# Blocks for B's input and for the compared matrices, and the order in which they are loaded, in a concatenated GFNet and FNet kernel

## The chip, the cores and the metric

The kernel runs on one core of a Trainium2 chip. The metric is device time in microseconds (us) of one launch; the median of three runs of the kernel before is 220.95 us (220.74 to 221.11). A profile is one further execution, taken by the hardware profiler; its instructions are counted from the start of its span.

Engine names are those of the profile: PE is the matrix engine, DVE the vector engine, ACT the scalar engine, POOL and SP the other two; SP issues most loads and stores here. Each engine works its instructions off in the order in which they were put, and an instruction that waits holds back those behind it. "PEld" is the loading of weights, "PEq" or "SPq" an engine's sequencer, where issues and waits stand.

## The reference

Two outputs are computed and put side by side (S = 2048, D = 512):

```
A:  X = rfft2(A_x);  y = irfft2(X * (w_r + i w_i))
B:  a = x @ hid_re.T;  b = x @ hid_im.T
    y = seq_re @ a - seq_im @ b
out = concat([A, B], axis=-1)
```

The four matrices of B (two of 2048 x 2048, two of 512 x 512) are inputs. The kernel takes B's output from fast Fourier steps, and reads the given matrices whole to compare them with tables of cosines and sines; only if they differ does it compute B from the matrices themselves, in a branch that is not taken here. Nearly half of all bytes that it moves, 33.6 MB, are those two large matrices ("C").

## The kernel before, in words

Three pieces of work are written as generators, and a loop at the end of the main function weaves them.

**A** (`a_work`) is the backbone; its yields count the steps n = 0 to 62.

- Steps 0 to 11, `forward`: eight loads of A's x (512 KB each) into the region `zv`; DVE adds and subtracts mirrored halves (`folded`, through the helper `TT`, line 233); PE transforms along the hidden axis (`hidden`, 32 matmul records for the first two, 16 for each later one), ACT copies (`taken`, line 481), PE transforms along 16 rows (`along`, 4 records each), ACT copies (line 488) into one of three buffers, and POOL stores them turned into `zv` (line 492, `turned`). A third-next copy has to wait until the store from its buffer has landed.
- Steps 12 to 38: eight slots (`slot`), each in four stages: the weights' load (POOL, line 302, issued behind the last turned store) and DVE sums `t` from `zv`; two transforms on PE with a table out of `slots`; five large DVE instructions; and four transforms back with copies into `zv` (line 592). A slot's first stage needs the turned stores landed. The first to run are slot 0's and slot 1's, at step 12.
- Steps 39 to 62, `inverse`: 128 matmul records for the hidden axis, 128 for the rows, ACT copies, and four stores `out_a` of 1 MB (line 626), two after each half.

**B** (`b_work`) has 27 steps, k = 0 to 26: 0 and 1 load x in four quarters of 1 MB, 2 to 9 are a fold on DVE (`b_fold`, four instructions) and 16 matmuls (`b_along`, four groups of rows) for each quarter in turn, 10 to 18 `b_hidden`, 19 to 26 `b_rows` with two stores of 256 KB each (a plain one from SP, an indexed one from POOL, line 432) out of two buffers `yb`. `B_AT[k]` is the step of A after which step k is written. Where k is in `PINNED`, its matmuls are put behind A's latest one on PE; its loads and DVE instructions are not.

**C** (`all_compared`) has 34 steps: 16 blocks, two steps for the hidden matrices (each with one block that ACT fills and one that is loaded), 16 blocks. A block is 1 MB in two loads (line 332), then one or two DVE instructions that compare and add up (`count`, line 317). The tables `tt` (1 MB each, line 327) serve eight blocks each; halfway through its eight blocks a table gets its sign turned on DVE (line 340). `C_AT` says for a block behind which step of A its count is put on DVE: behind the last `TT` of that step. In the loop of the kernel before, block i has the entry i - 1, and block 0 none; an entry of 0 is no pin. Loads are not pinned; each is issued when its place in SP's order and a free block allow.

x of B and C's blocks share six blocks (`XR = 6`, `block()`, line 304).

The order of each engine's instructions is fixed at compile time by a list scheduler, which takes what was written first wherever it counts it ready; so what is written later can be put into gaps of what was written earlier.

At the end DVE sums all counts (line 715), PE adds over partitions (717), DVE writes a flag (718) and all engines branch on it (720, 721).

Of the kernel before, what the change touches and what calls it, by code (L numbers as in the profile page):

```python
# [10 lines left out]
F32 = mybir.dt.float32  # L11
# [5 lines left out]
P = 128  # L17

YB = 2
XR = 6  # L20


B_AT = [0, 5, 7, 7, 8, 9, 9, 9, 9, 11, 13, 13, 13, 13, 13, 18, 20, 20, 21, 23, 27, 31, 31, 32, 50, 50, 50]
C_AT = [0, 0, 0, 3, 7, 12, 12, 12, 13, 34, 34, 38, 40, 40, 40, 40, 40, 40, 40, 40, 41, 41, 41, 44, 44, 44, 45, 45, 48, 48, 50, 59, 59, 59, 59, 61]
PINNED = [1, 2, 3, 4, 5, 6, 7, 8, 9, 10, 11, 12, 13, 14, 15, 17, 21]
SMALL = 2.0**-27
TINY = 2.0**-111

# [179 lines left out]
def kernel(  # L208
# [19 lines left out]
    nc = tc.nc  # L228
# [18 lines left out]
    bp = first.enter_context(tc.tile_pool(name="bp", bufs=1))  # L247
# [8 lines left out]
    slots = ap.tile([P, 2816], F32, name="slots")  # L256

    def short():
        return ap.tile([P, 6400], F32, name="zb")
# [13 lines left out]
    fb = bp.tile([P, 2, 272], F32, name="fb")  # L273
# [21 lines left out]
    def load(dst, src):  # L295
        loads.append(nc.sync.dma_start(dst, src))
        return dst

    def late(dst, src):

        with tc.issue_after(turned[-1].ins):
            nc.gpsimd.dma_start(dst, src)  # L302

    def block():
        return bp.tile([P, 4, 512], F32, name="xr", bufs=XR)

    hts = []
# [34 lines left out]
    def hidden_table():  # L342

        if not hts:
            hts.append(nc.sync.dma_start(ht, tabs["ht"]))
# [14 lines left out]

    def b_load(q):

        x = block()
        for k in range(4):
            g = 4 * q + k
            lo, hi = 1 + 4 * g, 124 - 4 * g
            load(x[:, k], bass.AP(xb.tensor, xb.offset + 16 * D * lo, [[D, 64], [16 * D * (hi - lo), 2], [1, D]]))
        if q == 3:
            load(x[1:32:2, 3], xb[0])
        return x  # L370
# [286 lines left out]

    def b_work():
        x = {0: b_load(0)}
        yield  # L660
        x.update({q: b_load(q) for q in range(1, 4)})
        nc.gpsimd.dma_start(fb, tabs["fb"])
        yield
        for q in range(4):
            ev = b_fold(x[q])
            yield
            for g in range(4 * q, 4 * q + 4):
                b_along(g, x[q], ev)
            if q == 0:
                nc.sync.dma_start(hc, tabs["hc"])  # L670
                nc.sync.dma_start(slots, tabs["slot"])
                hidden_table()
                nc.sync.dma_start(mb, tabs["mb"])
            yield
        z = short()
        zb = [part(z, 2 * k, 512) for k in range(9)]
        for e in range(9):
            b_hidden(e, zb)
            yield
        for o in range(8):  # L680
            b_rows(o, zb)
            yield
# [7 lines left out]

    count(same[:, 0:1], same[:, 1:2], TINY, ALU.is_equal)
    a, b, c = a_work(), b_work(), all_compared()
    done = []
    b_at, c_at = list(B_AT), list(C_AT)
    while b_at and b_at[0] < 0:
        b_at.pop(0)
        next(b)
    for n in range(100):
        if next(a, a) is a and not b_at:
            break  # L700
        while b_at and b_at[0] <= n:
            b_at.pop(0)
            k = len(B_AT) - len(b_at) - 1
            with tc.issue_after(mma[0].ins) if k in PINNED else ExitStack():
                next(b, None)
        done.append(last[0])
    for _ in b:
        pass
    for _ in c:
        n = c_at.pop(0) if c_at else 0  # L710
        pin[0] = done[min(n, len(done) - 1)] if n else None


    rs = bp.tile([P, 1], F32, name="rs")
# [124 lines left out]
```

## Time and profile before

| | |
|---|---|
| median of three runs | 220.95 us |
| the profiled execution | 220.61 us, of which its span 218.6 us |
| PE, DVE, ACT, POOL busy | 192.2, 158.9, 77.2, 39.2 us |
| moved by DMA | 69.68 MB, 319 GB/s over the span |
| mean granted PE clock | 0.929 |

What lies around the span (2.0 us in the profiled execution) is launch and end. A row of the timeline gives start, duration, engine, line, operation, tiles, shape and a count; in brackets the idle time of the engine before it and who ended that. A row of a group gives busy time and mean duration. A window row gives for each engine its busy time and number of instructions, then the granted clock, the DMA engines' busy share, and GB/s.

### The profile page before, as it was taken

How to read it: one execution, taken by the hardware profiler on the slowest of the kernel's cores; microseconds unless marked ns; L12 is line 12 of the kernel's file. 1: busy time of each engine (PE TensorE's matmuls, PEld its weight loads, DVE VectorE, ACT ScalarE, POOL GpSimd, SP SyncE). 2: the span in 40 equal slices, each digit the busy share in tenths (PEclk: the TensorE clock that was granted, in tenths of full speed). 3: DMA queues.
4: the chain of work that ended last, by engine and by line, in shares of the span. 5: the costliest groups of instructions: out<-in, count | busy, mean ns of one | idle time of the engine just before them, and what ended most of it. 6: DMA issues, size and time to landing. Idle time of an engine off the chain costs nothing. (4 is left out here: it accounts for less than half of the span.)

```text
span 218.6 us, 2541 instructions
## 1 busy us (share of the span) xinstructions
PE 192.2 (88%) x833; PEld 150.0 (69%) x833; DVE 158.9 (73%) x257; ACT 77.2 (35%) x159; POOL 39.2 (18%) x56
## 2 busy tenths in 40 slices
PE   7799999979959999999999967668999999999700
PEld 2687778858749576586866544466999998888600
DVE  1589400088684899999889979799994799989350
ACT  2034333083452224422416535447333133333300
POOL 4002220032270010232113443160050000000000
PEclk9999999999995699999999996767999999999985
DMA  6999999999999999972353274057899999999990
GB/s 215 389 408 387 379 401 403 404 408 390 381 387 384 385 408 406 391 231 89 116 194 105 97 280 178 16 189 288 338 418 411 416 408 407 410 411 420 388 393 13
DMA packets 20883, 69.68 MB, mean 319 GB/s; under 512 B 3616, under 2 KB 4000, under 8 KB 19456
## 3 DMA queue, kind: packets, MB, share of 16 engines
q1 hardware_dynamic: 16176, 58.05, 67.6%
q0 software_dynamic: 4400, 10.81, 14.1%
q10 hardware_dynamic: 288, 0.59, 0.7%
q8 instruction: 8, 0.13, 0.2%
q14 instruction: 11, 0.09, 0.1%
HBM read 56.85 MB, written 8.39 MB: 298 GB/s over the span
## 5 line engine op out<-in xcount | busy, mean ns | idle before, releaser
L317 DVE SCALAR_TENSOR_TENSOR xr<-xr,tt 128x1024 f32<-128x1024 f32 (+1 forms) x24 | 37.3, 1578 | 27.9 <-DMA xr<-in_cm 27.8
L317 DVE SCALAR_TENSOR_TENSOR xr<-xr,odd,tt 128x1024 f32<-128x1024 f32 (+1 forms) x24 | 38.7, 1637 | 6.0 <-DMA xr<-in_cm 6.0
L448 PE MATMUL pa<-ye,zv 128*128 128x256 f32 x128 | 30.3, 401 | 2.0 <-ACT zv L592 2.0
L448 PE MATMUL pa<-zb,sda 128*128 128x256 f32 x128 | 30.6, 395 | 1.4 <-DVE sda L233 1.4
L448 PEld LDWEIGHTS pa<-ye,zv 128*128 128x128 f32 x128 | 29.2, 306 | 3.0 <-ACT zv L592 2.3
L448 PEld LDWEIGHTS pa<-zb,sda 128*128 128x128 f32 x128 | 25.2, 199 | 8.6 <-DVE sda L233 2.3
L233 DVE TENSOR_TENSOR sda<-zv 128x512 f32<-128x512 f32 (+1 forms) x24 | 19.0, 821 | 12.8 <-DMA zv<-in_xa 7.2
L448 PE MATMUL pa<-ye,sda 128*128 128x256 f32 x128 | 27.8, 379 | 0.0
L448 PEld LDWEIGHTS pa<-ye,sda 128*128 128x128 f32 x128 | 24.3, 190 | 3.3
L448 PEld LDWEIGHTS pa<-slots,sda 128*128 128x128 f32 x128 | 19.6, 225 | 8.5 <-DVE sda L233 3.7
L448 PE MATMUL pa<-slots,sda 128*128 128x128 f32 (+1 forms) x128 | 21.2, 328 | 2.6 <-DVE sda L233 2.6
L233 DVE TENSOR_TENSOR sda<-sda 128x512 f32<-128x512 f32 (+1 forms) x34 | 22.9, 716 | 0.0
L492 POOL DMA_DIRECT2D zv<-zb x16 | 10.0, 631 | 48.7 <-ACT zb L488 32.9
L233 DVE TENSOR_TENSOR sda<-pa,sda 128x1024 f32<-128x1024 f32 (+1 forms) x16 | 17.8, 1152 | 0.5
L481 ACT COPY zb<-pa 128x1024 f32<-128x1024 f32 x8 | 8.1, 1012 | 25.8 <-PE pa L448 25.8
L432 POOL DMA_INDIRECT out_b<-yb,turn x8 | 12.4, 1554 | 25.0 <-ACT yb L422 23.9
L448 PE MATMUL pa<-zb 128*128 128x512 f32 x32 | 15.1, 598 | 1.2 <-ACT zb L481 1.2
L388 PE MATMUL pb<-fb,xr 128*128 128x128 f32 (+1 forms) x64 | 15.4, 327 | 0.5 <-DVE xr L233 0.5
L622 ACT COPY zv<-pa 128x512 f32<-128x512 f32 x16 | 9.4, 587 | 17.8 <-PE pa L448 17.8
L302 POOL DMA_DIRECT2D sda<-in_wa x16 | 11.4, 717 | 23.0 <-ACT zb L405 10.1
L388 PE MATMUL pb<-fb,yb 128*128 128x72 f32 x64 | 13.3, 295 | 2.4 <-DVE yb L233 1.4
L611 ACT COPY sda<-pa 128x1024 f32<-128x1024 f32 x8 | 8.1, 1016 | 19.2 <-PE pa L448 19.2
(83 smaller groups left out, 216.0 us busy)
## 6 DMA issues: line engine op xcount, KB each, us to landing
xr<-in_cm SPq DMA_DIRECT2D x64, 512.0 KB, 10.3
tt<-tab_tt SPq DMA_DIRECT2D x4, 1026.0 KB, 12.6
zv<-in_xa SPq DMA_DIRECT2D x8, 512.0 KB, 9.7
xr<-in_xb SPq DMA_DIRECT2D x16, 256.0 KB, 6.9
zv<-zb POOLq DMA_DIRECT2D x16, 256.0 KB, 8.4
sda<-in_wa POOLq DMA_DIRECT2D x16, 256.0 KB, 3.7
out_a<-zv SPq DMA_DIRECT2D x4, 1024.0 KB, 10.8
xr<-in_wd SPq DMA_DIRECT2D x2, 1024.0 KB
```

The source lines that it names most:

```text
L233: last[0] = nc.vector.tensor_tensor(**kw)
L302: nc.gpsimd.dma_start(dst, src)
L317: nc.vector.scalar_tensor_tensor(raw, raw, scale, v, op0=MUL, op1=op, accum_out=stat[:, i : i + 1])
L388: nc.tensor.matmul(bank[:, at : at + hi - lo], v[:, cols], f[:, lo:hi], start=True, stop=True)
L432: stores.append(nc.gpsimd.indirect_dma_start(out=out_b, out_offset=bass.IndirectOffsetOnAxis(ap=turn[:, o : o + 1], axis=0), in_=y[:, 1], ...
L448: mma[0] = nc.tensor.matmul(*args, **kw)
L481: nc.scalar.copy(zs[p], pd[p])
L492: turned.append(nc.gpsimd.dma_start(zv[at : at + 29 : 4], ys[:, k]))
L611: nc.scalar.copy(u[:, g : g + 2], pu)
L622: nc.scalar.copy(ob[:, c, :, :, g // 2], po.rearrange("p k r s -> p r k s"))
```

## The change

- Blocks: C's pool `xr` has four blocks, and a pool `xq` has two. B's x takes `xq` alone. From the 21st block that C asks for (count 20), every third (20, 23, 26, ...) comes from `xq` as well.
- B's loads: quarter 0 is loaded at step k = 0 (with the table `fb` on POOL's queue), quarter 1 at k = 1, quarters 2 and 3 after the matmuls of quarters 0 and 1. Steps k = 0 and 1 are written after A's steps 5 and 6 instead of 0 and 5.
- C: its first two steps (table 0, blocks 0 and 1) are written after A's step 0, so ahead of x of B, with no pin. Block i now has the entry i of `C_AT`.
- `slots` is loaded by the loop after step 6, ahead of quarter 1; it was among B's tables, which stay behind quarter 0's matmuls.
- All three lists are other ones.

```diff
-XR = 6
-B_AT = [0, 5, 7, 7, 8, 9, 9, 9, 9, 11, 13, 13, 13, 13, 13, 18, 20, 20, 21, 23, 27, 31, 31, 32, 50, 50, 50]
-C_AT = [0, 0, 0, 3, 7, 12, 12, 12, 13, 34, 34, 38, 40, 40, 40, 40, 40, 40, 40, 40, 41, 41, 41, 44, 44, 44, 45, 45, 48, 48, 50, 59, 59, 59, 59, 61]
-PINNED = [1, 2, 3, 4, 5, 6, 7, 8, 9, 10, 11, 12, 13, 14, 15, 17, 21]
+XR = 4
+XQ = 2
+EARLY = 2
+LENT = 20
+SLOTS = 6
+B_AT = [5, 6, 6, 13, 13, 13, 13, 14, 14, 15, 15, 17, 17, 22, 22, 24, 24, 25, 25, 29, 29, 33, 33, 33, 40, 44, 51]
+C_AT = [0, 0, 12, 12, 13, 14, 15, 15, 15, 22, 34, 34, 34, 34, 35, 35, 35, 37, 37, 37, 37, 37, 37, 37, 43, 43, 43, 43, 43, 43, 43, 43, 43, 43, 43, 43]
+PINNED = [0, 1, 2, 7, 11, 12, 13, 14, 15, 16, 17, 18, 19, 20, 21, 22, 24, 25, 26]
...
+    blocks = [0]
     def block():
+        i = blocks[0]
+        blocks[0] += 1
+        if i >= LENT and i % 3 == 2:
+            return bp.tile([P, 4, 512], F32, name="xq", bufs=XQ)
         return bp.tile([P, 4, 512], F32, name="xr", bufs=XR)
...
     def b_load(q):
-        x = block()
+        x = bp.tile([P, 4, 512], F32, name="xq", bufs=XQ)
...
     def b_work():
         x = {0: b_load(0)}
+        nc.gpsimd.dma_start(fb, tabs["fb"])
         yield
-        x.update({q: b_load(q) for q in range(1, 4)})
-        nc.gpsimd.dma_start(fb, tabs["fb"])
+        x[1] = b_load(1)
         yield
         for q in range(4):
             ev = b_fold(x[q])
             yield
             for g in range(4 * q, 4 * q + 4):
                 b_along(g, x[q], ev)
+            if q < 2:
+                x[q + 2] = b_load(q + 2)
             if q == 0:
                 nc.sync.dma_start(hc, tabs["hc"])
-                nc.sync.dma_start(slots, tabs["slot"])
                 hidden_table()
                 nc.sync.dma_start(mb, tabs["mb"])
             yield
...
+    early = 0
     for n in range(100):
         if next(a, a) is a and not b_at:
             break
+        if n == SLOTS:
+            nc.sync.dma_start(slots, tabs["slot"])
+        while early < EARLY and c_at[0] <= n:
+            c_at.pop(0)
+            early += 1
+            next(c)
         while b_at and b_at[0] <= n:
...
-    for _ in c:
+    while early < EARLY:
+        c_at.pop(0)
+        early += 1
+        next(c)
+    while True:
         n = c_at.pop(0) if c_at else 0
         pin[0] = done[min(n, len(done) - 1)] if n else None
+        if next(c, c) is c:
+            break
```

Each step k of B, with the step of A after which it is written:

| k | what | before | after |
|---|---|---|---|
| 0, 1 | loads of quarter 0; of 1 to 3 (after: of 1) | 0, 5 | 5, 6 |
| 2, 4, 6, 8 | folds | 7, 8, 9, 9 | 6, 13, 13, 14 |
| 3, 5, 7, 9 | matmuls of the quarters | 7, 9, 9, 11 | 13, 13, 14, 15 |
| 10 to 18 | `b_hidden` | 13 (five), 18, 20, 20, 21 | 15, 17, 17, 22, 22, 24, 24, 25, 25 |
| 19 to 26 | `b_rows` | 23, 27, 31, 31, 32, 50, 50, 50 | 29, 29, 33, 33, 33, 40, 44, 51 |

The counts' pins, by block: before, blocks 0 to 3 none, 4 step 3, 5 step 7, 6 to 8 step 12, 9 step 13, 10 and later step 34 and later. After: 0 and 1 none, 2 and 3 step 12, 4 step 13, 5 step 14, 6 to 8 step 15, 9 step 22, 10 and later step 34 and later. Step 12's last `TT` is in slot 1's sums `t`, step 34's in slot 7.

## The prediction

> **What bounds the kernel now.** I read the chain of waits first, to see what ends last, and then the engines by stretches of time.
>
> ```profile
> 163.16 11.49 DMA xr<-in_cm
> ...
> 195.32 12.45 DMA xr<-in_cm
> ...
> 207.88 2.40 DVE xr L317 x4
> ...
> 210.99 0.16 DVE flag L718
> ```
>
> The last 45 us are loads of C, one behind the other; the last lands at 207.8, its count ends at 210.28, the flag at 211.15. The span ends at 218.6, 7.45 us behind the flag. So C's last landing plus 10.8 us is the span. The same window holds A's inverse:
>
> ```profile
> 0.00:72.06 72.06, 65.21 (x296) 50.14 (x297) 35.45 (x59) 25.43 (x62) 15.45 (x28) 0.95 1.00 380
> 72.06:142.80 70.74, 65.06 (x265) 42.68 (x264) 65.37 (x122) 27.50 (x61) 17.91 (x26) 0.93 0.60 222
> 95.00:147.50 52.50, 45.80 (x202) 31.55 (x200) 47.74 (x91) 22.15 (x45) 18.09 (x22) 0.90 0.42 149
> 147.50:207.80 60.30, 57.89 (x256) 53.48 (x256) 50.59 (x64) 22.04 (x33) 3.00 (x1) 0.97 0.98 391
> 72.06 1.29 DVE L233 TENSOR_TENSOR sda<-zv 128x512 f32<-128x512 f32 x2 [3.81 <-issue]
> 142.72 0.18 DVE L233 TENSOR_TENSOR sda<-sda,sg 128x2 f32<-128x2 f32 x1
> 142.80 2.35 DVE L317 SCALAR_TENSOR_TENSOR xr<-xr,odd,tt 128x2048 f32<-128x2048 f32 x1
> ```
>
> The columns are PE, weight loads, DVE, ACT, POOL, clock, DMA share, GB/s. I split where DVE's work changes: 72.06 is the first slot sum, which needs A's turned rows; 142.80 is the end of the last slot's sums, where the counts that are pinned there start. Before 72 DMA is full (1.00) and DVE half idle. From 72 to 143, the slots, DVE is busy 65.37 of 70.74 us, PE 65.06, and from 95 on DMA only 0.42: all six blocks are full and nobody has counted them. Behind 147.5 DMA is at 0.98, 391 GB/s. So what happens after 142.8 is a fixed amount of traffic, and the time of the kernel hangs on when DVE has finished the slots. Call that S; S = 142.8, C's last landing is S + 65.0, the span S + 75.8.
>
> **What DVE has to do up to S, and when.**
>
> ```profile
> 23.04 1.30 DVE L233 TENSOR_TENSOR xr<-xr 128x1020 f32<-128x1020 f32 x2
> 44.67 2.29 DVE L317 SCALAR_TENSOR_TENSOR xr<-xr,tt 128x2048 f32<-128x2048 f32 x1 [20.34 <-DMA xr<-in_cm]
> 57.90 0.70 DVE L340 TENSOR_SCALAR tt<-tt 128x1024 f32<-128x1024 f32 x1
> L233 DVE TENSOR_TENSOR yb<-yb,pb 128x255 f32<-128x255 f32 x14 | 5.2, 414 | 2.6 <-ACT yb L419 2.6
> ```
>
> DVE stands idle for 20.3 us, from 24.3 to 44.67, because the first block of C queues behind x of B. By 142.8 it has done 35.45 + 65.37 = 100.8 us of work and idled 42.0. Within that: A's folds, four folds of B, blocks 0 to 9, the slots, and seven rows of B at 5.2 / 7 = 0.74 us. Ten blocks are counted by S in both versions (the pins of block 10 and later are at step 34 or later, those of 0 to 9 at 22 or earlier); of the rows of B, five instead of seven are written before step 34, which takes 1.5 us off: 99.3 us of work. S is then 99.3 us plus DVE's idle time, and as far as S decides, the change gains only if that idle time, 42.0 us now, stays below 43.5.
>
> The order does the opposite of what the first 20 us suggest. Before, blocks 0 to 5 are counted ahead of the slots (the pins are none, 3 and 7). After, only 0 and 1 are; 2 to 9 are pinned to step 12 or later, and step 12's last DVE sum is slot 1's, the instruction group at 72.06. So four counts of 2.35 us move from the idle stretch into the busy one, with one turn of a table's sign (0.70). Of the four folds of B (two rows like that at 23.04, 2.5 us), at least one moves too: quarter 2 is loaded only when quarter 0's matmuls have freed a block of the two, and quarter 3 after quarter 1. I take one, bounds one and two. The slots' stretch holds 65.37 - 1.5 + 4 x 2.35 + 0.70 + 2.5 = 76.5 us of DVE's work. Its idle time was 5.4 us; more counts are there to fill it, three rows of B in one step (33) on two buffers make some: 4.5 us, bounds 0 and 5.4. The stretch lasts 81.0 us instead of 70.7.
>
> **When the slots can start.** A's forward part no longer has matmuls of B written into it.
>
> ```profile
> 15.36 1.88 PE L448 MATMUL pa<-zb 128*128 128x512 f32 x4
> 17.08 3.62 PE L448 MATMUL pa<-zb,sda 128*128 128x256 f32 x16
> 20.53 1.88 PE L448 MATMUL pa<-zb 128*128 128x512 f32 x4
> 53.12 3.65 PE L448 MATMUL pa<-zb 128*128 128x512 f32 x8
> 47.26 3.54 POOL L492 DMA_DIRECT2D zv<-zb  x6 [17.15 <-ACT zb L488]
> 59.82 1.01 ACT L488 COPY zb<-pa 128x1024 f32<-128x1024 f32 x1 [0.71 <-DMA zv<-zb]
> 61.12 1.19 POOL L492 DMA_DIRECT2D zv<-zb  x2 [2.38 <-ACT zb L488]
> DMA to landing us min/median/max: 7.2/8.4/11.6
> ```
>
> The period is 20.53 - 15.36 = 5.17 us, and the last two of eight have no hidden part behind them: undisturbed, PE ends the forward part at 15.36 + 6 x 5.17 + 2 x 1.8 = 50.0 instead of 56.8. Then come a copy (1.0), two issues (1.2) and the landing of a turned store (last row, 7.2 to 11.6): 60.4 with the median of 8.4 and nothing in the way. But before, it took from 56.8 to 72.06, 15.3 us, because the fourth copy stood late in ACT's order (POOL idle for 17.15 us), and the last two copies then waited for buffers whose stores were on their way. That order comes from the compiler's belief on landings, which I can't see for the changed kernel; by the old lag the start is 65.3. The queue beside the turned stores is not shorter (behind A's x before: the four quarters; after: a table, two blocks, two quarters and the slots' tables), so I take 64.0, nearer to the old lag. This is 8 us earlier, and PE has quarters 0 and 1 of B to fill the gap behind 50. S becomes 64.0 + 81.0 = 145.0, later by 2.2 us. Bounds: 60.4 + 76.5 = 136.9, and 72.06 + 81.9 + 2.5 = 156.5 where a second fold moves and the turned rows are no earlier; the old lag gives 65.3 + 81.9 + 2.5 = 149.7.
>
> PE's work in the stretch is 65.06 less two rows of B and plus two quarters' matmuls:
>
> ```profile
> 120.03 1.02 PE L412 MATMUL pb<-zb,mb 128*128 128x512 f32 x2
> 206.58 0.59 ACT L622 COPY zv<-pa 128x512 f32<-128x512 f32 x1 [1.14 <-PE pa L448]
> L388 PE MATMUL pb<-fb,xr 128*128 128x128 f32 (+1 forms) x64 | 15.4, 327 | 0.5 <-DVE xr L233 0.5
> L388 PE MATMUL pb<-fb,yb 128*128 128x72 f32 x64 | 13.3, 295 | 2.4 <-DVE yb L233 1.4 <-ACT ye L393 1.1
> ```
>
> Half of line 388's 28.7 us is at most 14.4 (they overlap, so it is less): 65.06 - 2.0 + at most 14.4 = at most 77.5. DVE's 76.5 and PE's bound are near; I let DVE set it.
>
> **After S.** Blocks in hand are equal in number: before ten counted and six loaded, after ten counted, four in C's own pool, and blocks 20 and 23, which may be loaded as soon as B's quarters are done with the two blocks.
>
> ```profile
> 145.71 0.64 ACT L352 ACTIVATE xr<-ht 128x514 f32<-128x514 f32 x1
> 147.47 0.34 SPq L357 DMA_DIRECT2D xr<-in_wd  x1
> out_a<-zv SPq DMA_DIRECT2D x4, 1024.0 KB, 10.8
> xr<-in_cm SPq DMA_DIRECT2D x64, 512.0 KB, 10.3
> out_b<-yb SPq DMA_DIRECT2D x7, 256.0 KB, 2.0
> SPq L332 <- DVE xr L317: 23.4, 9, 8.5
> ```
>
> Before, the first block that was freed went to ACT (145.71), and the first load went out at 147.47, 4.7 us behind S; after, block 14's load can follow the first count, 2.35 us behind S: 2.3 us gained. Two more rows of B are stored behind S, 2 x 2 x 256 KB = 1.05 MB, at 391 GB/s 2.7 us. C's last landing is S + 65.4, the span S + 76.2 = 221.2. On PE the inverse starts as long behind S as before and gets three rows of B pinned into it (0.98 us each by the row at 120.03): its end moves from 207.2 to 207.2 + 2.2 + 2.9 = 212.3. Its last 2.1 MB take 5.4 us, to 217.7; before, they were through at 212.6, 6.0 us ahead of the span's end, of which I can't tell how much is needed. This gives at most 223.7. Between the two I take 221.7, as the chain before ended with the flag.
>
> The rest costs nothing that I can find. The first quarter of x comes later by what now stands ahead of it, a table and two blocks:
>
> ```profile
> tt<-tab_tt SPq DMA_DIRECT2D x4, 1026.0 KB, 12.6
> 36.04 0.34 PE L388 MATMUL pb<-fb,yb 128*128 128x72 f32 x2
> ```
>
> This is 3.1 MB or 7.9 us, but its matmuls were not begun before 36.04 and are now written for step 13; A's forward matmuls, until 50, are the cover, and without it the gap behind 50 would have less of B to fill it. hc, ht and mb stand behind quarter 2's load, which waits for quarter 0's matmuls; behind it in SP's order may stand C's blocks 2 and up as well. Their uses lie behind the slots' start, so up to some 10 us of waiting is free. `fb` stays on POOL ahead of the first turned store. The counts of blocks 0 and 1 are behind loads that no fold of A waits for.
>
> The profiled execution was 2.0 us longer than its span and 0.34 us below the median: 221.7 + 2.3 = **224.0 us**, 1.4% slower. Its own range, from idle time and start, is 221.5 to 228.
>
> **Rivals.**
>
> *The slots start early enough* (faster). If ACT's copies are not put late, the turned rows land at 60.4; with 1.5 us of idle time S = 60.4 + 76.5 + 1.5 = 138.4. By C the span is 214.6, by PE at most 217.1; at 215.6 the time is 217.9. For it: PE's forward part is 6.8 us shorter, and DVE's 20.3 us of idling shows that the old order of loads starved it. Against: the old lag, and DVE's extra 11 us in the stretch. It decides where start plus idle time in the stretch is below 65.9; my 64.0 + 4.5 is 2.6 above. Chance 0.32.
>
> *C's four blocks are too few* (slower still). Blocks 20 and 23 come early only if their loads are not behind waiting ones in SP's order. If they are, 14 blocks instead of 16 are in hand at S, and two blocks, 2.1 MB or 5.4 us, are added: 229.4. For it: SP already waits 23.4 us for DVE to free blocks. Against: before, SP's order has a table at 157.53 behind two blocks (four loads, at 154.37), where the code has it behind four, so a load may pass those that wait for a block. Chance 0.16.
>
> ```profile
> 154.37 3.11 SPq L332 DMA_DIRECT2D xr<-in_cm  x4
> 157.53 0.43 SPq L327 DMA_DIRECT2D tt<-tab_tt  x1
> ```
>
> The Trainium skill, "Perfetto Trace Analysis", section "Identifying the Most-Contended Engine", says that a gap that keeps coming back on the engine that should be saturated can mean too little SBUF for the next tile. By that rule alone, giving C four blocks for six speaks against this change, and the time would be this rival's 229.4. The trace agrees as far as DMA's 0.42 between 95 and 147.5 comes with SP waiting on DVE; but what is missing there is DVE's time and not room, since six blocks were full.
>
> *Nothing moves*: the earlier start and the longer stretch cancel within 0.4 us. A measurement here tells about 0.2%, or 0.44 us, from no change. Chance 0.08.
>
> **How the numbers follow.** The forecast has 0.44, the faster rival 0.32, the slower 0.16, no change 0.08. Slower by over 0.2% is 0.44 + 0.16 = 0.60. The range takes in most of the faster rival and most of the slower one: 215.5 to 230.
>
> **What would show it.** Right: DVE's count of block 0 near 21 to 24 instead of 44.67; the first slot sum near 64; eight counts between it and the last slot's sums; the stretch near 81 us with DVE above 92%; S near 145; C's last landing 65 behind S; blocks 20 and 23 loaded ahead of S. It is wrong if the stretch is no longer than 71 us, because counts of 2 to 9 were put behind S or DVE's idle time went elsewhere, or if the first slot sum comes before 60.

## The result, and the profile after

The changed kernel takes 234.09 us (median of four runs, 232.0 to 236.09), the kernel before 220.84 us beside it: a ratio of 1.058 (95% interval 1.0496 to 1.0664), slower. 1.4% were forecast, with 230 as the upper end of the range. The profiled execution took 234.05 us, its span is 231.4.

Ratios below are of each run to the kernel before on the same chip; a time that is given with one is the ratio times 220.9. Executions that took over 1.5% longer than the fastest of the same kernel are left out of the ratios, so a median of all runs can differ from that time; the profile of e6 is such an execution, and nothing is read from it.

The chain of waits of the changed kernel ends as before, with loads of C and their counts:

```profile
198.90 10.74 DMA xr<-in_cm
209.65 11.76 DMA xr<-in_cm
221.53 2.37 DVE xr L328 x2
```

Its windows, cut like those of before at the first slot sum, at S, and at C's last landing (PE, weight loads, DVE, ACT, POOL, clock, DMA share, GB/s):

```profile
0.00:79.76 79.76, 58.21 (x241) 40.82 (x241) 32.52 (x55) 22.96 (x44) 16.33 (x30) 0.91 0.93 346
79.76:150.77 71.01, 65.00 (x310) 46.72 (x310) 65.59 (x121) 25.58 (x70) 12.73 (x20) 0.93 0.53 185
150.77:221.41 70.64, 61.70 (x280) 56.10 (x280) 58.26 (x82) 28.98 (x46) 9.87 (x7) 0.97 0.98 392
```

S is 150.8 in place of 142.8. The slots last 71.0 us and hold 65.6 us of DVE's work, nearly what they held before (70.7 and 65.4). DVE has done 98.1 us of work by S (before 100.8) and idled 52.7 us (before 42.0). Behind S, 80.6 us follow in place of 75.8. So 8.0 us came before S and 4.8 behind it.

The idle time lies in front of the slots. DVE's timeline of the changed kernel (start, duration, in brackets the idle time before and who ended it):

```profile
21.87 2.29 DVE L328 SCALAR_TENSOR_TENSOR xr<-xr,tt 128x2048 f32<-128x2048 f32 x1 [3.22 <-DMA xr<-in_cm]
...
30.25 1.30 DVE L237 TENSOR_TENSOR yb<-xq 128x1020 f32<-128x1020 f32 x2 [3.66 <-DMA xq<-in_xb]
...
38.85 1.30 DVE L237 TENSOR_TENSOR yb<-xq 128x1020 f32<-128x1020 f32 x2 [6.05 <-DMA xq<-in_xb]
...
60.28 1.30 DVE L237 TENSOR_TENSOR yb<-xq 128x1020 f32<-128x1020 f32 x2 [18.88 <-DMA xq<-in_xb]
61.60 1.30 DVE L237 TENSOR_TENSOR xq<-xq 128x1020 f32<-128x1020 f32 x2
62.82 2.28 DVE L328 SCALAR_TENSOR_TENSOR xr<-xr,tt 128x2048 f32<-128x2048 f32 x1
...
71.56 1.30 DVE L237 TENSOR_TENSOR yb<-xq 128x1020 f32<-128x1020 f32 x2 [6.45 <-DMA xq<-in_xb]
...
77.48 2.35 DVE L328 SCALAR_TENSOR_TENSOR xr<-xr,odd,tt 128x2048 f32<-128x2048 f32 x1 [0.89 <-DMA xr<-in_cm]
...
79.76 1.29 DVE L237 TENSOR_TENSOR sda<-zv 128x512 f32<-128x512 f32 x2
...
81.23 2.35 DVE L328 SCALAR_TENSOR_TENSOR xr<-xr,odd,tt 128x2048 f32<-128x2048 f32 x1
```

Each of the four folds of B (30.25, 38.85, 60.28, 71.56) now waits for its quarter of x. The longest wait of before, 20.3 us for C's first block, is gone (21.87); one of 18.88 us for quarter 2 stands in its place, and more beside it. The waits of DVE in the first 100 us (us, times, longest), before and then after:

```profile
DVE xr L317 <- DMA xr<-in_cm: 24.1, 4, 20.3
DVE yb L233 <- DMA xr<-in_xb: 0.4, 1, 0.4
```

```profile
DVE yb L237 <- DMA xq<-in_xb: 35.0, 4, 18.9
DVE xr L328 <- DMA xr<-in_cm: 4.1, 2, 3.2
```

Where the quarters stand among SP's issues, before and then after (start, time from the first issue to the last, count):

```profile
7.76 15.54 SPq L296 DMA_DIRECT2D xr<-in_xb  x16
```

```profile
13.67 6.07 SPq L300 DMA_DIRECT2D xq<-in_xb  x4
...
21.77 5.04 SPq L300 DMA_DIRECT2D xq<-in_xb  x4
...
34.58 3.81 SPq L343 DMA_DIRECT2D xr<-in_cm  x4
38.75 0.33 SPq L338 DMA_DIRECT2D tt<-tab_tt  x1
39.20 4.55 SPq L343 DMA_DIRECT2D xr<-in_cm  x4
44.77 20.71 SPq L300 DMA_DIRECT2D xq<-in_xb  x9
65.57 1.96 SPq L343 DMA_DIRECT2D xr<-in_cm  x2
```

Before, all sixteen were issued by 23.3. After, quarters 2 and 3 stand behind C's blocks 2 to 5 and a table, and the ninth issue of the last group, the one row of quarter 3 (32 KB), is held until quarter 3 has landed: nothing behind it goes out until 65.57. SP's waits up to there name no matmul of B, so as far as the trace shows it is their place in SP's order that makes the two quarters late, and not a block of x still in use. The loads of C behind them have a second hold: they need a block that DVE frees with its count behind fold 2; that count ends at 65.1, and e16 below shows this hold by itself. Of C's four blocks, two hold blocks 2 and 3, whose first count starts at 81.23.

Behind S, the second difference: the indexed stores of the rows (times in ns, then the first and last start in us), before and after:

```profile
L432 POOL DMA_INDIRECT out_b<-yb,turn x8: 971/1104/2997, 120.6 to 159.6; - x8
```

```profile
L443 POOL DMA_INDIRECT out_b<-yb,turn x8: 971/1322/2262, 145.4 to 200.0; - x8
```

Of the 17 stores to `out_b`, 14 were issued ahead of S before, 5 after. By S 40.8 MB have moved in place of 43.1; at 392 GB/s the missing 2.3 MB are 5.8 us. This is an estimate, near the 4.8 us that are longer there; e12 and e14 below test it.

### The profile page after: what moved, and what is told of

Its sections match the earlier page's. It is cut to its first block, busy times and chain, and to the rows that moved or that the text cites. A ratio compares the mean times of both kernels' runs of the same rounds, so it can differ in the third digit from the quotient of the medians.

```text
span 231.4 us, 2549 instructions
## 1 busy us (share of the span) xinstructions
PE 185.5 (80%) x833; PEld 144.1 (62%) x833; DVE 159.1 (69%) x257; ACT 77.5 (34%) x159; POOL 38.9 (17%) x56
## 4 chain that ended last, share of the span: by engine, by line
DMA 52%; PE 19%; DVE 19%; issue 4%; ACT 1%; SPq 1%; DVEq 0%
DMA xr<-in_cm 33%; DVE xr L328 12%; PE pa L459 9%; DMA slots<-tab_slot 6%; DMA tt<-tab_tt 5%; DMA xq<-in_xb 4%; DVE sda L237 4%; PE pb L415 4%; DMA zv<-in_xa 3%; PE pb L411 2%; PE pb L412 1%; PE pb L413 1%; DMA out_b<-yb,turn 1%; DVE yb L237 1%; DVE xq L328 1%
## 5 line engine op out<-in xcount | busy, mean ns | idle before, releaser
L328 DVE SCALAR_TENSOR_TENSOR xr<-xr,odd,tt 128x1024 f32<-128x1024 f32 (+1 forms) x21 | 33.9, 1636 | 9.1 <-DMA xr<-in_cm 9.1
L459 PE MATMUL pa<-zb,sda 128*128 128x256 f32 x128 | 29.0, 381 | 3.1 <-ACT zb L499 1.6
L328 DVE SCALAR_TENSOR_TENSOR xr<-xr,tt 128x1024 f32<-128x1024 f32 (+1 forms) x18 | 27.8, 1573 | 3.2 <-DMA xr<-in_cm 3.2
L459 PEld LDWEIGHTS pa<-zb,sda 128*128 128x128 f32 x128 | 24.1, 190 | 9.0 <-DVE sda L237 2.4
L459 PE MATMUL pa<-ye,zv 128*128 128x256 f32 x128 | 28.9, 385 | 0.7 <-ACT zv L603 0.7
L237 DVE TENSOR_TENSOR yb<-xq 128x1020 f32<-128x1020 f32 (+1 forms) x8 | 5.2, 690 | 35.0 <-DMA xq<-in_xb 35.0
L459 PE MATMUL pa<-sda,slots 128*128 128x512 f32 x28 | 16.6, 726 | 8.5 <-DVE sda L237 8.5
L459 PEld LDWEIGHTS pa<-slots,sda 128*128 128x128 f32 x128 | 17.0, 191 | 4.3 <-issue 3.5
L459 PE MATMUL pa<-slots,sda 128*128 128x128 f32 (+1 forms) x128 | 17.8, 289 | 0.0
L459 PE MATMUL pa<-zv,slots 128*128 128x512 f32 x8 | 5.2, 814 | 12.8 <-DMA sda<-in_wa 12.8
```

The lines of the kernel that those rows point to most:

```text
L237: last[0] = nc.vector.tensor_tensor(**kw)
L328: nc.vector.scalar_tensor_tensor(raw, raw, scale, v, op0=MUL, op1=op, accum_out=stat[:, i : i + 1])
L459: mma[0] = nc.tensor.matmul(*args, **kw)
```

## The experiments

The theories: **E**, quarters 2 and 3 of x come late in SP's queue, and since DVE works its line off in order, their folds hold it; **A**, three counts stand ahead of the slots on DVE; **P**, the lists with their pins carry the loss. In the expectations B is the forecast's own picture (DVE's work plus its idle time set S), C says that PE decides, and L, from e12 on, that the new list of B puts the stores of its rows behind S. One table for all runs, worked out from each profile: the first slot sum, S, DVE's work and idle time by S, what follows S in the span, and the stores to `out_b` issued ahead of S.

| kernel | ratio (95%) | first sum | S | work | idle | span - S | stores |
|---|---|---|---|---|---|---|---|
| before | 1 | 72.1 | 142.8 | 100.8 | 42.0 | 75.8 | 14 |
| after | 1.058 (1.050-1.066) | 79.8 | 150.8 | 98.1 | 52.7 | 80.6 | 5 |
| e1 | 1.052 (1.046-1.058) | 71.9 | 151.1 | 98.2 | 52.9 | 80.2 | 5 |
| e2 | 1.067 (1.061-1.073) | 69.6 | 151.2 | 97.8 | 53.4 | 80.7 | 5 |
| e3 | 1.065 (1.058-1.073) | 79.2 | 150.5 | 98.1 | 52.4 | 80.8 | 5 |
| e4 | 1.007 (1.004-1.010) | 73.0 | 145.2 | 100.9 | 44.2 | 75.6 | 14 |
| e5 | 1.082 (1.077-1.087) | 90.7 | 156.7 | 98.7 | 58.0 | 80.2 | 5 |
| e6 | 1.025 (1.016-1.034) | | | | | | |
| e7 | 1.122 (1.112-1.132) | 85.1 | 166.7 | 99.8 | 66.9 | 80.7 | 9 |
| e8 | 1.040 (1.038-1.042) | 76.4 | 145.5 | 99.1 | 46.4 | 81.3 | 7 |
| e9 | 1.076 (1.073-1.080) | 81.1 | 153.6 | 98.8 | 54.8 | 81.2 | 7 |
| e10 | 1.041 (1.037-1.044) | 75.9 | 146.8 | 98.0 | 48.8 | 80.8 | 5 |
| e11 | 1.036 (1.034-1.039) | 78.2 | 145.2 | 98.7 | 46.5 | 81.4 | 5 |
| e12 | 1.029 (1.023-1.036) | 72.8 | 149.8 | 101.0 | 48.7 | 76.3 | 13 |
| e13 | 1.111 (1.106-1.117) | 81.0 | 153.6 | 98.4 | 55.2 | 88.0 | 5 |
| e14 | 1.050 (1.042-1.059) | 79.7 | 155.1 | 101.0 | 54.1 | 75.2 | 13 |
| e15 | 1.001 (0.998-1.003) | 71.3 | 142.6 | 100.8 | 41.8 | 75.7 | 14 |
| e16 | 1.053 (1.046-1.060) | 78.3 | 151.8 | 98.2 | 53.6 | 80.3 | 5 |
| e17 | 1.025 (1.019-1.031) | 75.2 | 146.2 | 100.7 | 45.5 | 76.1 | 14 |
| e18 | 1.081 (1.074-1.087) | 73.4 | 149.2 | 98.5 | 50.7 | 88.6 | 7 |

Two columns carry it. The work by S is 98 to 101 us everywhere, most where most of B's rows are done by then, so S moves mostly with the idle time. And the span behind S is near 75.7 us where 13 or 14 stores are issued ahead of S, and near 80.7 where 5 to 9 are; e13 and e18 are longer still. It is not the stores' bytes alone: e7, with 9 stores ahead, has as long a span behind S as the changed kernel with 5, and no run says why.

**e1, e2, e3: DVE's order and PE's pin.** The changed kernel with the counts of blocks 4 to 8 behind slot 1's sums; the same with fold 3 there too; and the changed kernel without the pin on quarter 2's matmuls.

```diff
-C_AT = [0, 0, 12, 12, 13, 14, 15, 15, 15, 22, ...
+C_AT = [0, 0, 12, 12, 12, 12, 12, 12, 12, 22, ...      # e1, e2
-            ev = b_fold(x[q])
+            with tc.issue_after(done[12].ins) if q == 3 else ExitStack():
+                ev = b_fold(x[q])                       # e2
-PINNED = [0, 1, 2, 7, 11, ...
+PINNED = [0, 1, 2, 11, ...                              # e3
```

> The changed kernel with one edit: the counts of blocks 4 to 8 get the pin 12 (slot 1's sums) in place of 13, 14, 15, which turned out to be folds of B; so on DVE counts 4, 5 and 6 stand behind slot 1's first sums instead of ahead. Theory A (the slots start late because DVE works off fold 3 and counts 5 and 6, which wait for loads, ahead of slot 1's sums): these sums come at about 74 instead of 79.8 (fold 3 is still ahead, its row lands at 71.4), PE's wait of 6.0 us between slot 0's and slot 1's transforms all but goes, the end of the slots' sums moves from 150.8 to about 145 and the time from 234.1 to about 228.5. Rival B (DVE's total of work and idle time decides, as the prediction had it): three counts only move into the stretch, DVE's idle time ahead of it grows by the 2.2 us of count 4; end of the sums 150 to 153, time 233 to 236. Rival C (PE decides: the matmuls of quarters 2 and 3 come late and PE stood idle for 12.8 us before slot 0): only PE's second wait goes, at most 6 us; the same as A for this run, told apart by the run with quarter 2's matmuls unpinned.

> As the run before it, and fold 3's DVE instructions put behind slot 1's sums as well. Theory A: the sums come as soon as the turned rows are there, at about 70 to 71, some 4 us earlier again, and the end of the slots' sums at about 141 to 143; time 225 to 227. Rival B: no gain over the changed kernel, 233 to 236. Rival C: quarter 3's matmuls come later than before by some 4 us, but PE has quarter 2's and slot 1's to do meanwhile; 228 to 231.

> The changed kernel with one edit: the matmuls of quarter 2 (step k = 7) are no longer pinned behind A's latest; on PE quarters 2 and 3 (32 matmuls) then stand ahead of slot 0's transform. Theory A: the slots' start is set by DVE and not by PE, so filling PE's gap ahead of slot 0 gains little: slot 0's transform has to wait for quarter 3's matmuls, until about 78, and slot 1's sums stay at about 79.8; time within 2 us of 234. Rival C: 14 matmul groups, some 7 us of PE's work, leave the stretch of the slots, in which PE is then no longer full; end of the slots' sums earlier by 4 to 7 us, time 227 to 230. Rival B: DVE's order is the same, 233 to 235.

None gains. In e1 the first slot sum comes at 71.9 in place of 79.8, and S does not move: the counts that stood in front of it now stand in the slots.

```profile
0.00:71.85 71.85, 54.58 (x233) 39.88 (x233) 25.62 (x46) 21.66 (x41) 14.96 (x28) 0.93 0.96 355
71.85:151.12 79.27, 68.25 (x318) 47.93 (x318) 72.57 (x128) 27.11 (x73) 15.23 (x22) 0.89 0.53 193
```

This is the forecast's own picture, 7 us of DVE's work more in a longer stretch, and it costs what the changed kernel costs. When the slots start does not decide; how long DVE has idled by S does. Theory A falls, and with e3, which gains nothing either, C.

**e4, e15: the early blocks alone, the slots' tables alone**, each added to the kernel before.

```diff
+        if n == 0:
+            next(c), next(c)                            # e4
-                nc.sync.dma_start(slots, tabs["slot"])  # e15
+        if n == 6:
+            nc.sync.dma_start(slots, tabs["slot"])      # e15
```

> The kernel before with one part of the change: its first two steps of C are written after A's step 0, so that table 0 and blocks 0 and 1 are loaded ahead of x of B; one pool of six blocks, lists and all else as before. Theory A and rival C: DVE's idle 20 us get two counts, x of B comes 8 us later, which delays folds 0 to 3 on DVE and the matmuls of quarters 0 to 3 only as far as PE and DVE had been waiting for nothing else; the slots start within 2 us of 72, time 219 to 222 (221 before): this part is harmless by itself. Rival B: two counts (4.7 us) fall into DVE's idle time; end of the slots' sums up to 4.7 us earlier, time 216 to 219. Rival D (loading C ahead of x of B is what costs): time 224 or more.

> The kernel before with one part of the change alone: the slots' tables loaded behind step 6 of A in place of behind B's first matmuls, which puts them ahead of hc in SP's order (and on the chip ahead of quarters 1 to 3 or behind them, as the scheduler places it). All theories: within 0.5% of before, since the first matmul of a slot waits for the turned data (72 us), and the tables land at 45 us there.

The two early blocks cost 0.7% there, 1.5 us, just above theory A's 222 and below D's 224; S comes 2.4 us later in the profiled execution, which took 0.5 us more than the median. The tables' place costs nothing.

**e5: the counts of blocks 2 to 5 unpinned** in the changed kernel, to free C's blocks early.

```diff
-C_AT = [0, 0, 12, 12, 13, 14, 15, ...
+C_AT = [0, 0, 0, 0, 0, 0, 15, ...
```

> The changed kernel with one edit: no pin for the counts of blocks 2 to 5 (entries 12, 12, 13, 14 become 0). The first four runs left the end of the slots' sums at 150.7 to 151.3 whatever stood ahead of slot 1's sums, which only theory B foresaw: that time is DVE's work plus its idle time. Theory B now says: blocks 2 to 5 have landed by 45 to 55 and lie there while DVE idles from 41 to 60; counted there they take some 8 to 10 us out of DVE's idle time of 52.7 us (before: 42); end of the slots' sums 141 to 144, and C's last landing as far behind it as in the changed kernel (70 us) or less; time 223 to 227. Rival E (loads of x of B in the two blocks, and SP's queue, set the pace, the counts can't help because fold 3 comes when it comes): end of the sums 149 or later, time 232 to 235.

It is slower than the change, and slower than either theory had it. SP's issues show why:

```profile
44.62 5.52 SPq L300 DMA_DIRECT2D xq<-in_xb  x4
50.93 4.56 SPq L343 DMA_DIRECT2D xr<-in_cm  x4
55.59 4.42 SPq L300 DMA_DIRECT2D xq<-in_xb  x4
61.65 6.10 SPq L343 DMA_DIRECT2D xr<-in_cm  x4
73.85 0.60 SPq L300 DMA_DIRECT2D xq<-in_xb  x1
```

Each block that is counted early lets another load of C into the queue, ahead of quarter 3 and of its row; fold 3 waits 19.18 us, until 81.39, and holds the slots behind it. Less waiting for blocks made more waiting for x.

**e6, e7: the pins alone and the pools alone**, in the kernel before: counts of blocks 2 to 8 behind step 12; and two pools with the late loads of quarters 2 and 3, lists as before.

```diff
-C_AT = [0, 0, 0, 3, 7, 12, ...
+C_AT = [0, 12, 12, 12, 12, 12, ...                      # e6
-XR = 6
+XR = 4; XQ = 2; LENT = 20                               # e7, with block() and b_load as in the change
-        x.update({q: b_load(q) for q in range(1, 4)})
+        x[1] = b_load(1)                                # e7
+            if q < 2:
+                x[q + 2] = b_load(q + 2)                # e7
```

> The kernel before with one edit: the counts of blocks 2 to 8 pinned behind slot 1's first sums (entries 12), as the change does with blocks 2 and 3; pools, load order and the rest as before. Theory B: four counts and a turn of a sign (10 us) leave the idle time ahead of the slots and come into the stretch; end of the slots' sums from 142.9 to about 150 to 153, time 228 to 232: the pins alone give most of the loss. Rival E: the pools' split and the late quarters of x are the cause, so this costs under 3 us: 220 to 224.

> The kernel before with one part of the change: two blocks for x of B and four for C, every third block from the 21st on from the two, quarters 2 and 3 loaded behind the matmuls of quarters 0 and 1; lists, and x of B ahead of C, as before. Theory B: DVE has C's blocks 20 us earlier, since two quarters fewer are ahead of them, so its idle time does not grow, but folds 2 and 3 come later and PE's forward part carries their matmuls pinned; end of the sums within 3 us of 142.9, time 219 to 224. Rival E: quarters 2 and 3 come late as in the changed kernel and the slots with them; time 228 or more.

The pins alone cost 2.5% (interval 1.6 to 3.4), 226.4 us: between the ranges of both theories, so this run decides for neither. The pools alone cost 12.2%, over twice the whole change. The old list writes B's matmuls into A's forward part, where they now meet late quarters, and A's turned stores, the last of which lands at 84.7 in place of 71.8, come late with them (POOL's waits in the first 100 us; it was 32.9 us in 5 waits before):

```profile
POOL zv L500 <- ACT zb L496: 46.2, 4, 21.7
```

The change as a whole, with new lists, early blocks and the tables' new place, is 14 us faster than this part alone (1.058 against 1.122). Early blocks and tables gain nothing by themselves (e4, e15), so it is likely, though not tested alone, that the new lists belong to the pools. A part measured alone is not its share of the whole.

**e8 to e10: one part at a time taken out of the change**: one pool of six with all quarters loaded at once (e8); one pool, quarters 2 and 3 where the change loads them (e9); no early blocks of C (e10).

```diff
-XR = 4
+XR = 6                                                  # e8, e9: x of B from block() again
-        x[1] = b_load(1)
+        x.update({q: b_load(q) for q in range(1, 4)})   # e8
-            if q < 2:
-                x[q + 2] = b_load(q + 2)                # e8
-EARLY = 2
+EARLY = 0                                               # e10
```

> The changed kernel with its lists, the two early blocks of C and the slots' tables where they are, but with before's one pool of six blocks, and all four quarters of x of B loaded at the step that loads quarter 1. Theory E (quarters 2 and 3 are loaded late because they wait for two blocks, and the folds hold VectorE for 35 us of such waits): quarter 2's and quarter 3's waits on VectorE fall from 18.9 and 6.5 us to under 5 together, B's last matmul along the sequence ends before 80 us instead of 94.6, and 222 to 228 us result; what is above 221 is the price of the counts that the new list holds behind step 12 and later. Rival P (the lists, with their pins, carry the loss, as in the kernel before with only its counts held, 227.9): 228 to 234, with S, the end of the last slot's sums, near 151 as there.

> The run with one pool of six blocks, but quarters 2 and 3 loaded behind the matmuls of quarters 0 and 1, as the changed kernel loads them. It parts the pool from the place of the two loads: there are six blocks, the first two of C and the four quarters take one each, so no quarter waits for a buffer. Theory E in its form 'the two blocks make the quarters wait': within 1.5 us of the run with one pool and all quarters at once. Form 'the program's place of the loads': 230 to 234. In both forms, the one-row load of quarter 3 still waits for quarter 3's load to land.

> The changed kernel with C's first two blocks loaded after x of B's first quarters, as all others of C are (the new pools, lists and the slots' tables stay). The two early blocks cost the kernel before 1.5 us when they alone were added. Theory E: the two blocks and their table are 3.1 MB in SP's queue ahead of x of B either way, because quarters 2 and 3 wait for their buffers; 232 to 235, no gain. Rival (the early blocks delay x of B's quarters 0 and 1, and with them all that follows): 3.66 and 6.05 us of VectorE's waits go, and 226 to 230 result.

e8 brings S back to 145.5, where e4 has it: S loses its 5.3 us by the pools and the late quarters, as theory E says. Its waits for x:

```profile
DVE yb L237 <- DMA xr<-in_xb: 9.4, 2, 7.3
```

But it is still 4.0% slower than before, all but 2.7 us of it behind S: B's matmuls end at 92.6 and not below 80 as theory E expected, since the list puts them at steps 13 to 15. Its 229.8 us is a time that only theory P named, with an S near 151 that did not come. So the lists do carry a part, behind S, and each theory was half right.

In e9 no quarter waits for a buffer, yet S is 153.6. The wait went elsewhere: 25.7 us for C in place of 9.6 in e8.

```profile
DVE xr L326 <- DMA xr<-in_cm: 25.7, 5, 14.0
```

In DVE's timeline, a count of C now stands ahead of fold 3, and fold 3 waits with it:

```profile
59.76 2.29 DVE L326 SCALAR_TENSOR_TENSOR xr<-xr,tt 128x2048 f32<-128x2048 f32 x1 [13.95 <-DMA xr<-in_cm]
```

So it is the place of the two loads in the program that costs (8 us of S against e8), not the small pool: with two pools in that place S is 2.8 us earlier. e10 refutes its first expectation: without the early blocks S is 4.0 us earlier and the time is 229.8. The 3.1 MB ahead of x of B cost 1.5 us with the old pools and 3.9 with the new ones; the waits for x fall from 35.0 to 25.7 us. That the first quarters, coming earlier, also bring the next two earlier is a likely reason, not a tested one.

**e11 to e14: which list.** e11 is e8 with blocks 2 to 5 counted early (the entries of before, moved by one block). e12 is e11 with B's lists of before, e13 is e11 with C's list of before. e14 is the changed kernel with only the hidden step's and the rows' places and pins taken from before.

```diff
+C_AT = [0, 0, 0, 3, 7, 12, 15, 15, 15, 22, ...          # e11, e12
+B_AT, PINNED: those of the kernel before                # e12
+C_AT = [0] + that of the kernel before                  # e13
+B_AT = [..., 15, 15, 15, 15, 15, 18, 20, 20, 21, 23, 27, 31, 31, 32, 50, 50, 50]   # e14, k = 10 and up
+PINNED = [0, 1, 2, 7, 10, 11, 12, 13, 14, 15, 17, 21]   # e14
```

> The run with one pool of six and all quarters at once, with the counts of C's third to sixth blocks at steps 0, 3, 7 and 12, as the kernel before has them, in place of 12, 12, 13 and 14. If the counts' pins are what is left of the loss there, this one is 2 to 6 us faster than the run with one pool alone, 220 to 223. If the order of B's steps (the other list) is what is left, it is within 1 us of that run.

> The run with one pool of six, all quarters at once and early counts (228.7), with the kernel before's list of steps and pins for B (B_AT, PINNED) in place of the changed one. Theory L (the new list puts the hidden step of B behind steps 15 to 25 and the rows behind 29 to 51, so that only 5 to 7 of the 17 stores of out_b start before S in place of 14; the 2 to 2.3 MB that move less by S cost 5.5 us behind it): 13 or 14 stores lie ahead of S, C's last landing is 66 us behind S in place of 71.5, and 221.5 to 224 us result. Rival (C's list, whose counts are spread otherwise from block 6 on, makes those 5.5 us): 227 to 230, with C's last landing still 71 us behind S.

> The counterpart: the run with one pool of six, all quarters at once, B's changed list, but C's whole list as before (each block behind the step it had there). Theory L: 227 to 230, no gain on 228.7, since the rows still fall behind S. Rival (C's list): 221.5 to 224.

> The changed kernel with both pools and the late quarters 2 and 3, in which only the places of the hidden step and of the rows of B are those of the kernel before (hidden at steps 13 to 21, here 15 to 21, rows at 23 to 50). Theory L: C's last landing comes 66 to 67 us behind S in place of 70.6 and the result is 226 to 231 if S stays near 151 to 153; the rest of the loss, 5 to 8 us, is S itself and stays. Rival (with x of B this late the rows can't come ahead of S, wherever the list puts them): S moves to 155 or later, and 232 to 237.

e11 is within 1 us of e8, so the new pins of blocks 2 to 5 cost nothing much in that place. In e12 theory L's stores are there, 13 ahead of S, and the span behind S falls from 81.4 to 76.3; but S grows by 4.6 us, and the time, 227.4, is one that only the rival named, whose 71 us up to C's last landing did not come. e14 does the same to the changed kernel, and this row is to be set beside the changed kernel's third window:

```profile
155.13:220.30 65.17, 58.30 (x272) 54.43 (x272) 55.36 (x74) 24.80 (x37) 3.23 (x2) 0.98 0.96 384
```

The traffic behind S is 5.5 us shorter, and S 4.3 us later, 2.9 of them DVE's own work; the ratios, 1.050 and 1.058, can't be told apart. S is where the rival had it, although the rows do come ahead of S (13 stores). Rows are not late for nothing: ahead of S their work lengthens the slots, behind S their stores lengthen the traffic. e13 is slower than any theory had it. Over e4, which has both lists of before, C's new list (from block 6 on) costs 5.0 us (e12), B's new one 23 (e13), and both 6.5 (e11), each with the tables' new places: what one list costs hangs on the other. How that comes about, above all the 88 us behind S in e13, stays open. The waits give one lead: from S to C's last landing, SP stands 13.5 us in e13 in front of stores of B's rows that wait for ACT's copies, against 3.4 in the changed kernel, and later loads of C stand behind them. No run tests it.

**e16, e17: the row of quarter 3.** Quarter 3's last load is split so that it leaves out the 16 partitions of the row, whose load then waits for nothing; in the changed kernel and in the kernel before.

```diff
+            if g == 15:
+                load(x[0::2, k], ...)      # 64 rows
+                load(x[33::2, k], ...)     # 48 rows
+                continue
```

> The changed kernel with the last load of quarter 3 in two loads that leave out the 16 partitions which the one-row load fills, so that the row's load has nothing to wait for and does not hold SP's queue (9.2 us there) and fold 3 (6.45 us of VectorE's wait). Theory E in its narrow form (this one load holds the queue, and with it C's loads and the last fold): S comes 3 to 6 us earlier than 151.0 and 227 to 231 us result. Rival W (VectorE's work in front of the slots is in one line, and the wait for quarter 2, 18.9 us, comes first; what fold 3 loses in waiting the counts behind it lose as well): S within 1.5 us of 151 and 232.5 to 235.

> The same edit in the kernel before, where the row's load is issued at 37.2 us behind C's first loads and two tables, and waits there for nothing long. Both theories: within 0.5% of before; if C's loads come any earlier for it, up to 1 us faster, and then it is the fastest version here.

In e16 fold 3 no longer waits, and the next in line waits in its place:

```profile
59.20 1.30 DVE L237 TENSOR_TENSOR yb<-xq 128x1020 f32<-128x1020 f32 x2 [18.09 <-DMA xq<-in_xb]
75.98 2.35 DVE L328 SCALAR_TENSOR_TENSOR xr<-xr,odd,tt 128x2048 f32<-128x2048 f32 x1 [7.00 <-DMA xr<-in_cm]
```

S is 151.8: the rival W was right, and the row is not the cause. SP's issues say more. With the row out of the way, C's next load still goes out only at 64.06, when DVE's count behind fold 2 (61.74 to 64.03) has freed a block:

```profile
64.06 23.44 SPq L343 DMA_DIRECT2D xr<-in_cm  x12
```

The loads of C wait for DVE's counts, DVE waits for a late quarter of x, and that quarter stood behind loads of C. e17 is 2.5% slower than before, where 0.5% at most was expected. Nothing waits for the row there, but the scheduler makes another order (that it does so because quarter 3 is complete earlier is not shown), in which the last of A's turned stores go out later (POOL's `zv<-zb` from 40 us on, first and last start at the end of the row; before, then e17):

```profile
L492 POOL DMA_DIRECT2D zv<-zb x10: 598/598/1048, 47.3 to 61.7; - x10
```

```profile
L496 POOL DMA_DIRECT2D zv<-zb x10: 596/596/988, 45.9 to 66.3; - x10
```

The slots start 3.2 us later with them, and S comes 3.4 us later.

**e18: four blocks for x of B and two for C.**

```diff
-XR = 4
-XQ = 2
+XR = 2
+XQ = 4        # quarters loaded as in e8; later blocks: i % 3 != 2
```

> The changed kernel with both pools kept, but four blocks for x of B (all quarters loaded at once) and two for C (later blocks of C take them in the same ratio, two of three from the pool of four). It parts the two halves of theory E: that quarters 2 and 3 come late, and that C streams through few blocks. If the late quarters carry the loss of S, S falls to 145 to 147, as with one pool of six (145.6), and 228 to 231 us result. If the number of blocks that C has matters as much, with two for C until the quarters are done, S stays at 150 or later and 233 or more result.

All quarters but the one row land by 44 us, and S is 149.2, not 145 to 147: with two blocks, only two counts are done ahead of the slots, and DVE stands idle in front of the first sum instead:

```profile
73.41 1.31 DVE L237 TENSOR_TENSOR sda<-zv 128x512 f32<-128x512 f32 x2 [14.98 <-DMA sda<-in_wa]
```

S gains 1.6 us where e8 gains 5.3: with early quarters but only two blocks for C, most of that gain is lost, so C's blocks matter too. Why 88.6 us follow S here stays open as well; SP's waits for the copies of B's rows are 12.2 us here. No version in this study beats the kernel before.

## Why the prediction was wrong

The frame held: S is DVE's work plus its idle time, the work was forecast as 99.3 us and is 98.1, and the end hangs on S. The direction came too, but not by the forecast's reason: it set a start 8 us earlier against a stretch 10 us longer, and neither came, so the sign is in part luck. Two terms are off. The forecast span was 221.7; S is 5.8 us later than 145.0, what follows S is 4.4 us longer than 76.2, and the 0.5 us added for PE was not needed: 221.7 + 5.8 + 4.4 - 0.5 = 231.4.

1. **"The rest costs nothing that I can find"** is the step that failed. It put the lateness of x of B at nothing, with A's forward matmuls on PE as the cover for the first quarter; for quarters 2 and 3 the sum has a fold's work in the stretch and no wait at all. The cover was looked for on the engine that uses the folds' result, PE; the fold is on DVE, and there it holds everything behind it. The waits for x went from 0.4 to 35.0 us; idle time by S was 52.7 in place of the 145.0 - 99.3 = 45.7 that the forecast implies. e8 shows 5.3 us of S to hang on the pools with their late quarters, e10 4.0 on the early blocks (the two overlap).
2. **The start of the slots**, 64.0, and **the stretch**, 81.0, came as 79.8 and 71.0. The prediction took every pin from step 12 on for one behind a slot's sums, which is wrong: after steps 13, 14 and 15 the last sum on DVE is a fold of quarter 2 or 3, not a slot's, so blocks 4 to 6 were counted behind those folds and ahead of the slots, and both late folds as well. The turned stores landed at 69.8 and did not decide. (The early bound of the start, 60.4, is 60.6 by its own terms; nothing hangs on it.) The errors, 15.8 and -10.0 us, partly cancel in S, and e1, which has the forecast's order, has the same S. The stretch of 71.0 us is the prediction's own sign of being wrong, by the second of its reasons: DVE's idle time went elsewhere, in front of the slots.
3. **Five rows ahead of S**: two were stored by then (5 stores of 17), and for three DVE's sums were done (two instructions each; the group in 79.76 to 150.8):

```profile
L237 DVE TENSOR_TENSOR yb<-yb,pb 128x255 f32<-128x255 f32 x6 | 2.2, 413 | 0.0
```

The forecast's "five instead of seven" set rows that are written ahead of step 34 in the new list against rows that DVE had done in the old kernel. By the lists both kernels write five there (before at 23, 27, 31, 31, 32): before, two of the rows written at step 50 ran ahead of S, and after, two of those written at 33 did not. The steps at 29 and 33 were taken for early enough; but the hidden step ended at 135.8 in place of 109.0, and rows come behind it. Three rows of 0.52 MB are 1.6 MB, at 392 GB/s 4.0 of the 4.4 us.
4. **After S**, the restart came as forecast, the first load 2.4 us behind S (2.35 forecast). Blocks 20 and 23 were loaded ahead of S, at 89.7 and 95.0, so the rival "four blocks are too few" was wrong in its place. In its cause it had a point: C's blocks lay uncounted in front of the slots (81.23), and e18 shows that fewer still cost more. The rule that the prediction cited beside it (the Trainium skill, "Perfetto Trace Analysis", where it stands in the section "Optimization Strategy") spoke against giving C fewer blocks. e8, with six again and the quarters loaded at once, has 4.6 us less of span, but e9, with six and late quarters, has 3.4 us more: room alone was not what was missing.
5. The faster rival needed start plus idle time in the stretch below 65.9; they came as 79.8 + 5.4.

By spans, along one path of runs, the loss of 12.8 us is: the early blocks 2.2 (e4), the lists 6.0, nearly all of it behind S (e8 against e4), the two pools with their late quarters 4.6 (changed kernel against e8); by the ratios it is 1.5, 7.4 and 3.9. The lists' share takes in the tables' new places. By another order of taking parts out the shares differ, as e7 and e10 show.

## What to carry to other kernels

When a load is moved back, look for its cover on the engine that waits for it first, and count what is queued behind the waiting instruction; an engine that works in order waits for whichever supply is last, so here one wait removed came back as the next (e5, e16). When the work up to a point is fixed, its idle time is the only thing to argue about: sum up every wait in front of it, not the largest one. A list of places and pins fits the buffers that it was made with: parts of such a change can't be priced alone and added up.

## What was not expected of the hardware

A 32 KB load behind loads into the same tile held SP's queue: it went out at 64.88, when the last of quarter 3's loads had landed (64.86), and the loads of C behind it at 65.57; SP waited 9.2 us for it. Taking this away gained nothing (e16), as the loads of C then waited for a block until 64.06. In the kernel before it lost 2.5% (e17), where the trace shows another order of ACT's copies and POOL's stores.
